# Spectral mixing and a gated FFN on one core: six table transfers put ahead of the weight loads, and row 8's fillers split

## The chip, the cores and the metric

The kernel runs on one core of one Trainium2 chip. The metric is the device time of one execution in microseconds (us), taken as the median of several runs. A profiled execution gives the trace: every instruction of the engines PE (matmuls, with the weight loads on PEld), DVE (VectorE), ACT (ScalarE) and POOL (GpSimd), and the issues of the DMA queue SP, on one clock that starts with the span.

## The reference

```python
def _A_ref(x, w_r, w_i):                       # x: 1 x 2048 x 576
    X = rfft2(x.astype(float32), axes=(-2, -1))
    X = X * (w_r + 1j * w_i)
    return irfft2(X, s=(S, D)).astype(bfloat16)

def _B_ref(x, w_gate, w_up, w_down):           # 576 -> 4608 -> 576
    return (gelu(x @ w_gate) * (x @ w_up)) @ w_down

h  = x + _A_ref(layernorm(x), w_r, w_i)
h2 = h + _B_ref(layernorm(h), w_gate, w_up, w_down)
```

Inputs and output are bfloat16. The Fourier transforms are done as matrix products with tables of sines and cosines that the kernel makes itself.

## The kernel before

The order of the instructions on every engine is the order of the source: nothing is rescheduled. Each engine works through its own list and waits, instruction by instruction, for what it reads and for the tile that it writes. The 2048 tokens lie in the 16 rows h of `h_sb` (128 partitions each). PSUM is used as four tiles of two banks each, taken in rotation (`two(name)`): a new tile waits until the readers of the tile four takes earlier are done.

The work falls into these stages:

1. **Rows.** DVE and ACT take the statistics of the 16 rows (`sd`, `ln_act`), POOL the reciprocal roots, DVE normalises a row into `xn` (L137), PE multiplies it with the row table `F16` (`row16`, L308, and `row16_rest`, L324). ACT and DVE cast the products from PSUM to `Bt` (`evict`, L335; `evict4`, L341). `small_table` (L404) makes a small PSUM tile `pt` out of `F16` and the identity; ACT copies it to `G16` later (L447), for use near the end of the spectral part. Ahead of rows 0 and 8 `row16` calls `fill`: matmuls of the identity with the first row of `h_sb` (L298), written to the PSUM bank that the row then overwrites. Nobody reads their result.
2. **Columns, and the way back along the tokens.** A loop over i, with the frequencies k in `order`: `f2` (L516) multiplies `Bt` with the column table `DT`, ACT casts the result (L527), `f3` (L533, L534) combines, DVE sums (`sum_of`, L566) and multiplies with the weights of the filter (`wmul`, L584 to L608) into `Zt`, and `i3` (L624, for k = 0 L648) transforms back along the tokens with the table `TI`, from where ACT (L632, L637, L656, L661) and in one place DVE (L656) write `EO`.
3. **Back along the columns.** `inv_cols(x, g)` (L675) multiplies `EO[x]` with the inverse column table: five steps w, each with two matmuls, one on the partitions from 0 up and one on those from 64 up. The latter read `DQ[64:, w]`, the former `DQ[0:, w]`, but for w = 0, where they read `DT` itself. ACT takes most of the results out (L692, L699), DVE two (L690, L697). `add_rows` (L811) adds the parts to rows of `h_sb`.
4. **The FFN.** `gate` (L939) multiplies the normalised rows with gate and up weights, then the down product (L982, L1001) follows, four times over 512 tokens. The first groups of weights, `pre`, are loaded while stage 2 runs.

All the transfers that the change speaks of go through one queue, SP, which issues them in the order of the source. `load_dq(1)` (seven transfers, SBUF to SBUF, source `DT`) fills the upper half of `DQ` at the end of stage 1. `load_dq(0)` (six transfers of 6.8 to 32.9 KB) fills the lower half; its call stands in the branch i = 2 of the loop of stage 2, in this order:

```python
cosine(rest)                                    # ACT
turn_tf(rest)                                   # SP: transposes TF into TI (L269)
pre = [load_gu(g) for g in range(3)]            # SP: wgu, six loads of 432 KB (L146)
load_dq(0)                                      # SP: six transfers (L484)
nc.sync.dma_start(wd_a[:], ...)                 # SP: 1728 KB (L734)
```

The next loads on SP are `wgu_e` (four of 432 KB), whose memory comes free when the last `i3` has read its tables.

On PE the last part of stage 2 and the first of stage 3 are interleaved: f3(0), inv_cols(0, 0) and (0, 1), i3(6), inv_cols(0, 2) to (0, 4), i3(7), inv_cols(0, 5) and (0, 6), i3(0), inv_cols(0, 7), inv_cols(1, 0) and so on (`order` is 1 to 7, then 0).

Of the kernel before, what the change touches and what calls it, by code (L numbers as in the profile page):

```python
# [42 lines left out]
def kernel_body(  # L43
# [23 lines left out]
    def two(name):  # L67
        return psum.tile([P, 2, 512], FP32, name=name, tag="two", bufs=4)
# [72 lines left out]
    def load_gu(g, t=None):  # L141
        gc = slice(g % (NFT // FQ) * FQ * P, (g % (NFT // FQ) + 1) * FQ * P)
        if t is None:
            t = wgpool.tile([P, NR, FQ * P], BF16, name="wgu", tag="wgu")[:]
        for c, w in ((0, B_w_gate), (1, B_w_up)):
            nc.sync.dma_start(t[64 * c : 64 * c + 64], w[:, gc].rearrange("(r k) c -> k r c", k=64))  # L146
        return t
# [105 lines left out]
    def angle_s(sl):  # L253
        V.tensor_scalar(ab[:, sl], pr[:, sl], -1024.0, None, op0=ALU.add)

    def angle_c(sl):
        drop_sign(ab[:, sl], ab[:, sl])

    def sine(sl):
        A.activation(TF[:, sl, 2, :], pr[:, sl], ACT.Sin, bias=pib[:], scale=-2.0 * PI / S)  # L260

    def cosine(sl):
        A.activation(TF[:, sl, 1, :], ab[:, sl], ACT.Sin, bias=nhpib[:], scale=2.0 * PI / S)

    def minus_sine(sl):
        V.tensor_scalar(TF[:, sl, 0, :], TF[:, sl, 2, :], -1.0, None, op0=ALU.mult)

    def turn_tf(sl):
        nc.sync.dma_start(  # L269
            TI[:, sl].rearrange("p k r q -> p (k r) q"), TF[:, sl].rearrange("p k r q -> p (k r q)"), transpose=True  # L270
        )
# [18 lines left out]
        V.tensor_scalar(F16[:, 2, :], F16[:, 0, :], -1.0, None, op0=ALU.mult)  # L290

    ps_f = {}
    FILL = {0: 16, 8: 12}

    def fill(dst, n):

        for _ in range(n):
            T.matmul(dst, lhsT=ident[:], rhs=h_sb[:, 0, 0:512], start=True, stop=True)  # L298

    def row16(h):  # L300
        if h % 2 == 0 or h == H - 1:
            ps_f[h] = two("f2t")
        f2t, b = (ps_f[h], 0) if h in ps_f else (ps_f[h - 1], 1)
        fill(f2t[:, b, :], FILL.get(h, 0))
        x = xn[:, h, :]
# [92 lines left out]
    pt = []  # L398

    def small_table():  # L400
        pt.append(two("pt"))
        for x in range(2):
            for p0 in (0, 64):
                T.matmul(  # L404
                    pt[0][p0 : p0 + 64, 0, x * P : (x + 1) * P],
                    lhsT=F16[:, 0, 64 * x : 64 * x + 64],
                    rhs=ident[:],
                    start=True,
                    stop=True,
                )  # L410
# [24 lines left out]
    norms(4, 8)  # L435
    rests(4)
    small_table()
    gather(1)
    sd(10, 12)
# [38 lines left out]
    def load_dq(r):  # L478
        for w in range(1 - r, NW):
            j0, j1 = w * JW, (w + 1) * JW  # L480
            for lo, hi in ((j0, min(j1, (j0 // P + 1) * P)), ((j0 // P + 1) * P, j1)):
                if lo < hi:
                    p0 = 64 * r + lo - j0
                    nc.sync.dma_start(  # L484
                        DQ[p0 : p0 + hi - lo, w], DT[lo % P : lo % P + hi - lo, lo // P, :, r, :]
                    )
# [22 lines left out]
    def f2(c):  # L509
        ps = two("pq_ps")  # L510
        col = slice(slot[c] * P, (slot[c] + 1) * P)
        steps = [(par, t) for par in range(2) for t in (par, par + 2, 4)]
        if c == order[0]:
            steps.sort(key=lambda s: s[1] == 4)
        for par, t in steps:
            T.matmul(  # L516
                ps[:, par, 0:JP],
                lhsT=Bt[:, t, col],
                rhs=DT[:, t // 2, par] if t < 4 else DF[:, par],
                start=(t == par),  # L520
                stop=(t == 4),
            )
        pq[c] = wk.tile([P, 2, JP], BF16, name="pq", tag="pq", bufs=6)
        pq_ps[c] = ps

    def f2_out(c, copy=A.copy, rs=slice(0, 2)):
        copy(  # L527
            pq[c][:, rs].rearrange("p r (j a) -> p r j a", a=2),
            pq_ps[c][:, :, 0:JP].rearrange("p a (r j) -> p r j a", r=2)[:, rs],
        )  # L530
# [5 lines left out]
    def f3(k, half):  # L536
        ps = two("gh_ps")
        if k == 0:
            p0, p8 = pq[0], pq[8]
            t0, t1 = (NS, C) if half else (C, SN)  # L540
            for b, kk, p in ((0, 0, p0), (1, 8, p8)):
                comb(ps[:, b, 0:J], kk, t0, p[:, 0, 0:J], t1, p[:, 1, 0:J])
            if half == 0:
                xab[k] = wk.tile([P, 2, 2, JP], BF16, name="xab", tag="xab", bufs=2)
            A.copy(xab[k][:, half, :, 0:J], ps[:, :, 0:J])
            return
        p, q = pq[k], pq[k + 8]
        gh = wk.tile([P, 2, JP], BF16, name="hs" if half else "g", tag="hs" if half else "g", bufs=2)
        r = half
        comb(ps[:, r, 0:J], k, C, p[:, r, 0:J], SN, q[:, r, 0:J])  # L550
        comb(ps[:, 1 - r, 0:J], k, C, q[:, r, 0:J], NS, p[:, r, 0:J])
        if k == order[0] and half:
            hk[k] = ps
            return
        A.copy(gh[:, :, 0:J], ps[:, :, 0:J])
        if half == 0:
            gk[k] = gh
            return
        hk[k] = gh

    def sum_of(k, half):
        g, hs = gk[k], hk[k]
        if half == 0:
            xab[k] = wk.tile([P, 2, 2, JP], BF16, name="xab", tag="xab", bufs=2)
        x = xab[k]
        V.tensor_tensor(  # L566
            x[:, 1, ::-1, 0:J] if half else x[:, 0, :, 0:J],
            g[:, :, 0:J],
            hs[:, :, 0:J],
            ALU.add if half else ALU.subtract,  # L570
        )
# [133 lines left out]
    for i in range(n + 1):  # L705
        last = i >= n
        if not last:
            f2(order[i])
            if i != 1:
                f2_out(order[i])  # L710
        if i == 0:
            f2(order[0] + 8)
            for r in range(2):
                f2_out(order[0] + 8, V.tensor_copy, slice(r, r + 1))
            angle_s(rest)
            angle_c(rest)
            sine(rest)

        if 1 <= i <= n:
            f3(order[i - 1], 0)  # L720
            f3(order[i - 1], 1)
            if i == 1:
                f2_out(order[1])
                minus_sine(rest)
                sum_of(order[0], 0)
                sum_of(order[0], 1)
                V.tensor_scalar(G16v[1], G16v[0], -1.0, None, op0=ALU.mult)
            else:
                if i == 2:
                    cosine(rest)  # L730
                    turn_tf(rest)
                    pre = [load_gu(g) for g in range(3)]
                    load_dq(0)
                    nc.sync.dma_start(wd_a[:], wd_view[:, 0:NWA, :])  # L734
                wmul(order[i - 2], i - 1, order[i - 1])
        if not last and i:
            f2(order[i] + 8)
            f2_out(order[i] + 8)
        if last:
            inv_cols(0, 0)  # L740
            inv_cols(0, 1)
        if i >= 3:
            for s in range(3):
                i3(order[i - 3], s)
        if last:
            wmul(order[i - 1], i)
        if i == 2:
            scr_pool.__exit__(None, None, None)
            eop = ctx.enter_context(tc.tile_pool(name="eop", bufs=1, side="right"))
            EO = [eop.tile([P, 5, H, 2, 4, 8], BF16, name=f"EO{x}", tag=f"EO{x}") for x in range(2)]  # L750
# [266 lines left out]
@with_exitstack  # L1017
def kernel(
    ctx: ExitStack,
    tc: tile.TileContext,  # L1020
    A_x: bass.AP,
    A_w_r: bass.AP,
    A_w_i: bass.AP,
    B_x: bass.AP,
    B_w_gate: bass.AP,
    B_w_up: bass.AP,
    B_w_down: bass.AP,
    out: bass.AP,
):
    kernel_body(tc, A_x, A_w_r, A_w_i, B_x, B_w_gate, B_w_up, B_w_down, out)  # L1030
# [30 lines left out]
```

## Time and profile before

| | |
|---|---|
| median of 3 runs | 503.55 us (502.54 to 503.64) |
| profiled execution, its time | 503.53 us |
| its span, first to last instruction | 501.7 us |
| mean granted TensorE clock | 0.992 |
| PE busy | 489.0 us |
| DVE, ACT, POOL busy | 223.9, 160.0, 28.3 us |
| first FFN matmul (L939) | at 74.19 us |

A line of the timeline reads: start in us, busy time in us, engine, source line, operation, output and inputs, shape, count; in square brackets the idle time of the engine ahead of it and what ended it. Several instructions of one kind in a row are merged into one line. SPq is SP's queue as it issues transfers: the landing is later.

### The profile page before, as it was taken

How to read it: one execution, taken by the hardware profiler on the slowest of the kernel's cores; microseconds unless marked ns; L12 is line 12 of the kernel's file. 1: busy time of each engine (PE TensorE's matmuls, PEld its weight loads, DVE VectorE, ACT ScalarE, POOL GpSimd, SP SyncE). 2: the span in 40 equal slices, each digit the busy share in tenths (PEclk: the TensorE clock that was granted, in tenths of full speed). 3: DMA queues.
4: the chain of work that ended last, by engine and by line, in shares of the span. 5: the costliest groups of instructions: out<-in, count | busy, mean ns of one | idle time of the engine just before them, and what ended most of it. 6: DMA issues, size and time to landing. Idle time of an engine off the chain costs nothing.

```text
span 501.7 us, 12760 instructions
## 1 busy us (share of the span) xinstructions
PE 489.0 (97%) x5714; PEld 340.9 (68%) x5714; DVE 223.9 (45%) x450; ACT 160.0 (32%) x284; POOL 28.3 (6%) x79
## 2 busy tenths in 40 slices
PE   7799799999999999999999999999999999999997
PEld 3578489886569975555589955555799655555995
DVE  7999566599751237633311155333212233333111
ACT  8899574332220113323210032323100232323000
POOL 8400000011110001100000000000000000000000
PEclk9999799999999999999999999999999999999999
DMA  8649566949993019987750069988700188770000
GB/s 277 209 88 205 158 137 160 194 100 198 198 230 69 1 50 173 192 160 160 159 104 2 3 130 189 205 155 159 154 5 3 53 164 159 158 151 6 13 14 24
DMA packets 89549, 62.33 MB, mean 124 GB/s; under 512 B 23190, under 2 KB 88086, under 8 KB 89494
## 3 DMA queue, kind: packets, MB, share of 16 engines
q1 hardware_dynamic: 89206, 60.34, 59.4%
q0 software_dynamic: 288, 1.18, 0.8%
q8 instruction: 44, 0.72, 0.6%
q14 instruction: 11, 0.09, 0.1%
HBM read 52.65 MB, written 2.36 MB: 110 GB/s over the span
## 4 chain that ended last, share of the span: by engine, by line
PE 89%; SPq 3%; DMA 1%; issue 0%; DVE 0%
PE gu L939 56%; PE acc L982 26%; PE cs_ps L675 2%; SPq L484 2%; PE acc L1001 2%; SPq L146 1%; PE y_ps L811 1%; PE eo_ps L624 1%; DMA DQ<-DT 1%; PE eo_ps L648 0%; PE pt L880 0%; PE pq_ps L516 0%; PE gh_ps L534 0%; DVE h_sb L1008 0%; SPq L269 0%
## 5 line engine op out<-in xcount | busy, mean ns | idle before, releaser
L939 PE MATMUL gu<-Bt,wgu 64*128 64x512 bf16 (+1 forms) x2646 | 270.6, 363 | 0.0
L939 PEld LDWEIGHTS <-wgu 64*128 64x128 bf16 x2646 | 152.5, 94 | 114.6 <-issue 0.3
L948 DVE TENSOR_TENSOR P_sb<-g_sb,gu 128x512 bf16<-128x512 f32 (+1 forms) x156 | 100.4, 645 | 140.3 <-ACT g_sb L947 140.3
L947 ACT ACTIVATE g_sb<-gu 128x512 f32<-128x512 f32 (+1 forms) x156 | 88.0, 564 | 193.5 <-PE gu L939 193.5
L982 PEld LDWEIGHTS <-P_sb 64*128 64x128 bf16 x2160 | 123.1, 94 | 9.9
L982 PE MATMUL acc<-wd,P_sb 64*128 64x288 bf16 x1440 | 90.9, 283 | 0.0
L991 DVE TENSOR_TENSOR part<-part,acc 128x576 f32<-128x576 f32 x15 | 11.3, 755 | 112.6 <-ACT part L990 112.6
L990 ACT COPY part<-acc 128x576 f32<-128x576 f32 x15 | 9.6, 639 | 122.8 <-PE acc L982 122.8
L982 PE MATMUL acc<-wd_a,P_sb 64*128 64x288 bf16 x720 | 46.8, 283 | 0.0
L675 PE MATMUL cs_ps<-DQ,EO 58*128 58x290 bf16 x144 | 13.4, 315 | 2.7 <-DMA DQ<-DT 2.7
L298 PE MATMUL f2t<-h_sb,ident 128*128 128x512 bf16 x28 | 9.2, 498 | 5.4 <-DMA h_sb<-in_A_x_dram 3.7
L675 PEld LDWEIGHTS <-EO 58*128 58x128 bf16 x160 | 8.4, 103 | 7.1 <-issue 3.4
L516 PE MATMUL pq_ps<-DT,Bt 128*128 128x290 bf16 x64 | 12.3, 286 | 1.0 <-ACT Bt L335 1.0
L939 PE MATMUL gu<-Bt,wgu_e 64*128 64x256 bf16 (+1 forms) x162 | 12.5, 305 | 0.0
L836 DVE TENSOR_SCALAR hrow<-h_sb,mv,rstd 128x1152 bf16<-128x1152 bf16 x14 | 12.2, 868 | 0.6 <-POOL rstd L874 0.6
L516 PEld LDWEIGHTS <-Bt 128*128 128x128 bf16 x96 | 9.2, 97 | 3.5 <-ACT Bt L335 1.1
L993 DVE TENSOR_TENSOR h_sb<-h_sb,part 128x576 bf16<-128x576 bf16 x15 | 11.4, 758 | 0.5
L134 POOL TENSOR_TENSOR rstd<-rstd,mhalf 128x1 f32<-128x1 f32 (+1 forms) x16 | 11.2, 699 | 1.3
L939 PEld LDWEIGHTS <-wgu_e 64*128 64x128 bf16 x162 | 10.3, 94 | 1.2
L133 POOL TENSOR_SCALAR rstd<-mv 128x1 f32<-128x1 f32 (+1 forms) x16 | 3.9, 243 | 116.9 <-DVE mv L119 115.9
L298 PEld LDWEIGHTS <-ident 128*128 128x128 bf16 x28 | 3.4, 121 | 10.3 <-issue 6.3
L527 ACT CAST pq<-pq_ps 128x580 bf16<-128x580 f32 x15 | 9.9, 666 | 0.4 <-PE pq_ps L516 0.2
(143 smaller groups left out, 283.6 us busy)
## 6 DMA issues: line engine op xcount, KB each, us to landing
wgu<-in_B_w_gate_dram SPq DMA_DIRECT2D x46, 432.0 KB
wgu<-in_B_w_up_dram SPq DMA_DIRECT2D x46, 432.0 KB
wd_a<-in_B_w_down_dram SPq DMA_DIRECT2D x1, 1728.0 KB
wd<-in_B_w_down_dram SPq DMA_DIRECT2D x1, 1728.0 KB
wd<-in_B_w_down_dram SPq DMA_DIRECT2D x6, 288.0 KB
out_dram<-h_sb SPq DMA_DIRECT2D x3, 576.0 KB
h_sb<-in_A_x_dram SPq DMA_DIRECT2D x4, 288.0 KB
h_sb<-in_A_x_dram SPq DMA_DIRECT2D x2, 576.0 KB
```

The source lines that it names most:

```text
L134: G.tensor_tensor(dst[:, sl], dst[:, sl], mhalf[:, sl], ALU.pow)
L298: T.matmul(dst, lhsT=ident[:], rhs=h_sb[:, 0, 0:512], start=True, stop=True)
L484: nc.sync.dma_start(DQ[p0 : p0 + hi - lo, w], DT[lo % P : lo % P + hi - lo, lo // P, :, r, :])
L516: T.matmul(ps[:, par, 0:JP], lhsT=Bt[:, t, col], rhs=DT[:, t // 2, par] if t < 4 else DF[:, par], start=(t == par), stop=(t == 4),)
L675: T.matmul(ps[:, e, 0:JP], lhsT=EO[x][rows, w, 2 * g : 2 * g + 2].rearrange("p h e k l -> p (h e k l)"), rhs=DQ[rows, w] if w or e else DT ...
L836: V.tensor_scalar(hrow[:], h_sb[:, h, :].rearrange("p (r k) -> p r k", k=64).unsqueeze(2).to_broadcast([P, NR, 2, 64]), mv2[:, h, 0:1], rs ...
L939: T.matmul(gu[:, c, 0:n], lhsT=w[rows, r, i * P : (i + 1) * P], rhs=hl[tcnk % 2][rows, r, lo:hi], start=(r == 0), stop=(r == NR - 1),)
L947: A.activation(g_sb, gu[:, 0, 0:n], ACT.Gelu_apprx_tanh)
L948: V.tensor_tensor(p_sb(f)[:, lo:hi], g_sb, gu[:, 1, 0:n], ALU.mult)
L982: T.matmul(accs[i][:, c, 0:DH], lhsT=p_sb(f)[rows, st * P : (st + 1) * P], rhs=wd[f // NWA][rows, f % NWA, c * DH : (c + 1) * DH], start=( ...
L991: V.tensor_tensor(part, part, accs[1][:, :, 0:DH], ALU.add)
L993: V.tensor_tensor(hv, hv, part, ALU.add)
```

## The change

Two edits that are independent of each other. `load_dq(0)` is called ahead of the three `load_gu` instead of behind them, so on SP the six transfers L484 stand directly behind the transposes of `turn_tf(rest)`, and the six loads of `wgu` behind them; `wd_a` follows as before. And row 8's twelve fillers become nine: six are called in `small_table`, written to the second bank of `pt` ahead of the four matmuls L404 (which use the first bank), and three stay ahead of row 8. Nothing else moves on any engine; the lines behind the first edit have numbers higher by one.

```diff
-    FILL = {0: 16, 8: 12}
+    FILL = {0: 16, 8: 3}
...
     def small_table():
         pt.append(two("pt"))
+        fill(pt[0][:, 1, :], 6)
         for x in range(2):
             for p0 in (0, 64):
                 T.matmul(
...
                     cosine(rest)
                     turn_tf(rest)
+                    load_dq(0)
                     pre = [load_gu(g) for g in range(3)]
-                    load_dq(0)
                     nc.sync.dma_start(wd_a[:], wd_view[:, 0:NWA, :])
```

## The prediction

> **What bounds the kernel now.** I read four views in this order: the chain that ended last, the waits of PE, the granted clock by stretches, and the timelines of the engines around the two edits. First the chain (start, duration, what):
>
> ```profile
> 51.59 2.88 DMA DQ<-DT
> ...
> 61.44 1.20 PE eo_ps L624 x10
> ...
> 63.99 1.24 PE eo_ps L648 x40
> ...
> 68.19 3.74 PE cs_ps L675 x60
> ...
> 74.45 27.46 PE gu L939 x468
> ```
>
> From 74.45 us on the FFN's matmuls are the chain, nearly without a break. Neither edit touches them, so all that can be won is that they begin sooner. Ahead of them the chain runs through a transfer of `DQ`: PE waited for the table's lower half. PE's own waits from 10 to 76 us (total, times, longest) and the stretches (length; then for PE, PEld, DVE, ACT, POOL the busy time; granted clock, DMA share, GB/s):
>
> ```profile
> PE cs_ps L675 <- DMA DQ<-DT: 2.7, 4, 1.6
> PE f2t L298 <- ACT Bt L335: 1.7, 1, 1.7
> PE pq_ps L516 <- ACT Bt L335: 1.0, 1, 1.0
> ```
>
> ```profile
> 14.20:18.80 4.60, 2.89 (x22) 1.43 (x18) 4.53 (x18) 3.67 (x6) 3.70 (x9) 1.00 0.86 295
> ...
> 32.40:50.40 18.00, 17.97 (x151) 14.57 (x150) 18.00 (x41) 17.18 (x30) 0.00 (x0) 1.00 1.02 187
> 50.40:54.50 4.10, 1.38 (x10) 0.41 (x8) 3.96 (x10) 1.33 (x3) 0.00 (x0) 0.91 0.45 80
> 54.50:61.00 6.50, 6.49 (x48) 3.81 (x50) 2.09 (x4) 3.77 (x6) 0.00 (x0) 0.53 0.71 249
> ```
>
> The waits for `DQ` sum to 2.7 us, but the price is larger. In the thin stretch from 50.40 to 54.50 PE is busy for 1.38 of 4.10 us, and the clock, 1.00 before, is 0.91 over it and 0.53 over the next 6.50 us, in which PE is full: it works there at half speed. Wait and slow clock together are the price, and I take it from the schedule, not by adding the two.
>
> **Edit 1, the six transfers.** The issues on SP (start, time taken to issue):
>
> ```profile
> 26.82 5.35 SPq L484 DMA_DIRECT2D DQ<-DT  x7
> 32.28 3.21 SPq L269 DMA_TRANSPOSE TI<-TF  x1
> ...
> 42.08 10.16 SPq L484 DMA_DIRECT2D DQ<-DT  x6
> ```
>
> [...] The seven of the upper half, with no weights ahead, took 5.35, or 0.76 each. In the new place they start when the transposes are issued, 32.28 + 3.21 = 35.49, take 6 x 0.76 = 4.6, and with the 2.88 of the chain behind the last issue they land at about 43; if they issued as slowly as now, at 48.5. PE first asks for them at 50.46 (below), so the cover is 2 to 7 us, and I cost them at nothing. They need nothing that is late: `DT` was last written in stage 1. What queues behind them on SP are the six loads of `wgu` and `wd_a`, each 4.6 us later; the rivals return to that.
>
> What is late next? Without the wait three engines could set the pace from 50.46 to the first `inv_cols(1, 0)`, which stands at 65.79 now:
>
> ```profile
> 50.46 0.29 PE L675 MATMUL cs_ps<-DQ,EO 58*128 58x290 bf16 x1
> ...
> 65.79 0.28 PE L675 MATMUL cs_ps<-DT,EO 58*128 58x290 bf16 x1
> ...
> 83.03 3.21 PE L939 MATMUL gu<-Bt,wgu_e 64*128 64x256 bf16 x54
> ```
>
> ```profile
> 50.52 1.21 ACT L545 CAST xab<-gh_ps 128x578 bf16<-128x578 f32 x2
> ...
> 62.45 1.01 ACT L632 CAST EO<-eo_ps 128x1024 bf16<-128x1024 f32 x1 [0.28 <-PE eo_ps L624]
> ...
> 63.63 0.72 ACT L692 ACTIVATE cw<-cs_ps 128x580 f32<-128x580 f32 x1
> 64.60 0.59 ACT L656 CAST EO<-eo_ps 128x512 bf16<-128x512 f32 x1 [0.25 <-PE eo_ps L648]
> 65.27 0.37 ACT L661 CAST EO<-eo_ps 128x256 bf16<-128x256 f32 x1
> ...
> 66.62 0.83 ACT L699 ACTIVATE cs<-cs_ps 128x580 bf16<-128x580 f32 x1
> ...
> 70.28 2.98 ACT L692 ACTIVATE cwb<-cs_ps 128x580 f32<-128x580 f32 x5
> ```
>
> PE at full clock: eight `inv_cols` at 3.74 / 6 = 0.62, two `i3` at 1.20, one at 1.24, together 8.6, so 50.46 + 8.6 = 59.1. ACT, which must empty these tiles in order: `xab` 1.21, two `cs` at 0.83, two pairs L632 and L637 at 63.63 - 62.45 = 1.18, four `cw` at 2.98 / 5 = 0.60, L656 0.59 and L661 0.37, together 8.6, so 50.52 + 8.6 = 59.1. DVE hands over the last `Zt` at 56.70 (its row is in the next part), after which 1.24 of `i3` and 0.62 of `inv_cols` follow, 58.6. PE and ACT end together; as PE also waits for one of four PSUM tiles now and then, I take 59.2. Edit 1 is worth 65.79 - 59.2 = 6.6 us. Its bounds: 7.2 if PE and ACT are a little shorter in a stream than in these rows, so that DVE's 58.6 sets the end, and 5.9 if handing over from PE to ACT and back costs another 0.1 at each of seven places.
>
> **Edit 2, the fillers.** The rows of PE, DVE and ACT in stage 1:
>
> ```profile
> 14.23 0.30 PE L404 MATMUL pt<-ident,F 128*64 128x128 bf16 x4
> 16.24 2.75 PE L298 MATMUL f2t<-h_sb,ident 128*128 128x512 bf16 x12 [1.71 <-ACT Bt L335]
> 18.83 1.91 PE L308 MATMUL f2t<-F,xn 128*128 128x256 bf16 x16
> ...
> 22.86 0.41 PE L324 MATMUL f<-F,xn 128*64 128x128 bf16 x8
> 24.27 0.67 PE L516 MATMUL pq_ps<-DT,Bt 128*128 128x290 bf16 x4 [0.99 <-ACT Bt L335]
> ```
>
> ```profile
> 17.06 1.40 DVE L137 TENSOR_SCALAR xn<-h_sb,mv,rstd 128x576 bf16<-128x576 bf16 x4
> ...
> 19.49 1.44 DVE L137 TENSOR_SCALAR xn<-h_sb,mv,rstd 128x576 bf16<-128x576 bf16 x4
> ...
> 22.07 0.31 DVE L463 COPY DF<-DT 32x580 bf16<-32x580 bf16 x1
> 23.32 0.69 DVE L341 CAST Bt<-f 128x512 bf16<-128x512 f32 x1 [0.94 <-PE f L324]
> ...
> 56.24 0.46 DVE L608 TENSOR_TENSOR Zt<-m,m 128x580 bf16<-128x580 bf16 x1
> ```
>
> ```profile
> 17.46 0.41 ACT L447 ACTIVATE G<-pt 128x256 bf16<-128x256 f32 x1
> 19.90 1.93 ACT L335 CAST Bt<-f2t 128x1024 bf16<-128x1024 f32 x2 [2.03 <-PE f2t L308]
> ...
> 22.19 2.02 ACT L335 CAST Bt<-f2t 128x1024 bf16<-128x1024 f32 x3
> ```
>
> A filler costs (18.83 - 16.24) / 12 = 0.216. Six of them now stand at 14.23, where the tile `pt` is free (the table's matmuls start there today), and end at 15.5, the table at 15.9. ACT copies `pt` only at 17.46, so the delay of 1.3 costs nothing. The remaining three wait, as the twelve did, for row 8's PSUM tile until 16.24 and end at 16.9. Row 8 needs its `xn`, the first of four at 17.06 + 0.35, so PE starts it at 17.5 and not at 18.83: the last six fillers were no cover, they held the row up for 1.3. From there: rows 8 to 11 and their rests 1.9 + 0.4 to 19.8; row 12's `xn` comes at 19.49 + 0.36, so it starts at 19.95 and the last rest ends at 22.2, now 22.86 + 0.41 = 23.27. DVE's cast L341 then waits for DVE alone, 22.07 + 0.31 = 22.38, and starts at 22.4 for 23.32: 0.9 of the idle 0.94. ACT casts row 8 at 18.5, and its last cast follows row 15 (21.9): with the three casts spread over the rows and 2.02 / 4 for a single one, it ends at 23.0 for 24.2. So `f2` could start 1.1 sooner, but the angles, the first `pq` halves and all sums behind L341 are DVE's, which has no gap from 32.40 to 50.40 (18.00 busy of 18.00). The smaller figure passes: 0.9 up to the last `Zt`, `turn_tf(rest)` and the six transfers included. Bounds: 0, if another input of stage 2 is as late as L341, and 0.94, DVE's whole idle; I take 0.9, nearest to the row. Below 0 I see nothing: no instruction is added, three are gone, and none moves behind a later one.
>
> **The sum.** 6.6 + 0.9 = 7.5 us off the profiled execution's 503.53 us (span 501.7, so 1.8 outside it, unchanged): 496.0. The median, 503.55, is the same within 0.02. FFN start: 74.2 - 7.5 = 66.7.
>
> **Rivals.** *Only edit 1 counts:* 503.5 - 6.6 = 496.9. For it: stage 2 starts off several inputs at once. Against: the 0.94 in DVE's row is its only idle time there that a row on PE ends.
>
> *The clock falls all the same.* With the wait gone, PE, ACT and four PSUM tiles cycle at equal pace, with short idles on PE; a thin stretch could again halve the clock. One cold stretch of the length seen (about 6.8 us: from the end of 50.40:54.50, where 0.91 leaves 0.7, to 61.0 less 0.4) costs half of it, 3.4: 499.4. Against: from 32.40 to 50.40 the same four tiles cycle with ACT busy for 17.18 of 18.00, at 1.00; and at 14.20:18.80, with PE busy for only 2.89 of 4.60, the clock held too. [...] I give it 0.05.
>
> *The table is late anyway.* If the six stick behind the transposes in the queue, PE waits again, and only edit 2 and a part remain: 499 to 502.6 (503.5 - 0.9). It decides if they take more than 2 to 7 us longer than I reckon. Against: the upper half also followed transposes, and its first part was there at 50.46 without a wait.
>
> *Slower: the weights are late.* `wgu` and `wd_a` (six of 432 KB, 1728 KB) now start 3.7 later (4.6 less 0.9), and `wgu_e` (four of 432 KB) queues behind them. All are 6.2 MB; at the 187 GB/s of 32.40:50.40 that is 33 us from 39.2, so 72.3. The first use of `wgu_e` moves from 83.03 to 75.5: 3 us of slack, more since one of its two groups is enough to start. To end over 504.5, the transfers must land 8.5 us after that use, at 84, a rate of 138 GB/s. Against: 249 GB/s stood at 54.50:61.00. 0.03.
>
> **Chances and range.** Forecast 0.80; only edit 1 0.08; clock 0.05; table late 0.03; weights late 0.03; nothing moves, 503.5, 0.01. The forecast's own bounds run from 503.5 - 7.2 - 0.94 = 495.4 to 503.5 - 5.9 - 0.6 = 497.0; the runs' spread of 1.1 adds half a microsecond at each end, and with the first rival at 496.9 that makes 494.9 to 497.9, 0.88 of the cases less what the spread leaves out. The measurement can tell about 0.2%, 1.0 us. Faster by more: all but two of the cases, 0.95; the same 0.02; slower 0.03.
>
> **What would show it.** Right: in the profile after, L485's six issues stand directly behind the transposes and take about 4.6 us; PE has no wait for `DQ`; the clock is 1.00 from 50 to 61; L308 for row 8 starts near 17.5, DVE's cast L341 near 22.4; `inv_cols(1, 0)` at 58.3, the first L940 at 66.7. Wrong: a wait of PE on ACT of over 1 us in stage 3, a clock of half there, a wait of PE for `wgu` or `wgu_e`, or L341 at its old place.

## The result, and the profile after

The changed kernel takes 496.37 us (median of 4 runs, 495.88 to 496.45) against 503.58 before (4 runs); the ratio is 0.9859, 95% interval 0.9842 to 0.9877. Beside 16 runs of the kernel before on one chip it took 496.28 against 502.69, ratio 0.9871 (0.9856 to 0.9886). The forecast was 496.0, with 494.9 to 497.9 as its range. The profiled execution's span went from 501.7 to 494.6 us.

These are all the waits of PE from 10 to 70 us after (total in us, times, longest). The wait for `DQ` is gone, and nothing is left of the wait of the fillers for ACT:

```profile
PE f2t L308 <- DVE xn L137: 1.6, 3, 0.9
PE pq_ps L517 <- ACT Bt L335: 0.9, 1, 0.9
PE gh_ps L534 <- ACT TF L263: 0.3, 1, 0.3
PE gh_ps L535 <- ACT pq L528: 0.2, 1, 0.2
```

The stretches after are set 0.9 us earlier than those shown of before (length; busy time of PE, PEld, DVE, ACT, POOL; granted clock, DMA share, GB/s). PE is full, and at clock 1.00. Before it was busy for 1.38 of 4.10 us there and then ran at a mean of 0.53 over 6.50 us:

```profile
49.50:53.60 4.10, 4.10 (x55) 2.90 (x55) 3.96 (x9) 4.10 (x9) 0.00 (x0) 1.00 1.13 203
53.60:60.00 6.40, 6.40 (x116) 4.87 (x112) 3.79 (x7) 5.69 (x10) 0.00 (x0) 1.00 1.08 308
```

The issues on SP after. The six stand directly behind the transposes and take 4.44 us for 10.16; the first weight load starts at 39.75:

```profile
31.72 3.49 SPq L269 DMA_TRANSPOSE TI<-TF  x1
35.26 4.44 SPq L485 DMA_DIRECT2D DQ<-DT  x6
39.75 0.70 SPq L146 DMA_DIRECT2D wgu<-in_B_w_gate_dram  x1
```

PE in stage 1 and at the end of the spectral part, then DVE and ACT. The small table follows the six fillers at 15.81, three more fillers start at 16.14, and row 8 now waits for DVE alone:

```profile
14.41 1.47 PE L298 MATMUL pt<-h_sb,ident 128*128 128x512 bf16 x6
15.81 0.30 PE L405 MATMUL pt<-ident,F 128*64 128x128 bf16 x4
16.14 0.81 PE L298 MATMUL f2t<-h_sb,ident 128*128 128x512 bf16 x3
17.81 1.92 PE L308 MATMUL f2t<-F,xn 128*128 128x256 bf16 x16 [0.86 <-DVE xn L137]
...
23.42 0.67 PE L517 MATMUL pq_ps<-DT,Bt 128*128 128x290 bf16 x4 [0.87 <-ACT Bt L335]
```

```profile
49.66 0.29 PE L676 MATMUL cs_ps<-DT,EO 58*128 58x290 bf16 x1
...
58.62 0.28 PE L676 MATMUL cs_ps<-DT,EO 58*128 58x290 bf16 x1
...
67.00 9.11 PE L940 MATMUL gu<-Bt,wgu 64*128 64x256 bf16 x162
```

```profile
17.38 1.40 DVE L137 TENSOR_SCALAR xn<-h_sb,mv,rstd 128x576 bf16<-128x576 bf16 x4
...
22.73 0.69 DVE L341 CAST Bt<-f 128x512 bf16<-128x512 f32 x1
...
55.59 0.46 DVE L609 TENSOR_TENSOR Zt<-m,m 128x580 bf16<-128x580 bf16 x1
```

The first `inv_cols(0, 0)` starts at 49.66 for 50.46, `inv_cols(1, 0)` at 58.62 for 65.79, the FFN at 67.00 for 74.2. Between the first two points lie 8.96 us after and 15.33 before. These 6.37 us come from edit 1, and the 0.80 us by which the first point moved from edit 2, as the kernels with one edit alone bear out below.

### The profile page after: what moved, and what is told of

It is laid out like the page before. It is cut to its first block, busy times and chain, and to the rows that moved or that the text cites. A ratio compares the mean times of both kernels' runs of the same rounds, so it can differ in the third digit from the quotient of the medians.

```text
span 494.6 us, 12754 instructions
## 1 busy us (share of the span) xinstructions
PE 484.7 (98%) x5711; PEld 338.8 (69%) x5711; DVE 224.2 (45%) x450; ACT 159.2 (32%) x284; POOL 29.0 (6%) x79
## 4 chain that ended last, share of the span: by engine, by line
PE 93%; DVE 0%; issue 0%
PE gu L940 57%; PE acc L983 27%; PE cs_ps L676 2%; PE acc L1002 2%; PE eo_ps L625 2%; PE pq_ps L517 1%; PE y_ps L812 1%; PE gh_ps L535 1%; PE gh_ps L534 1%; PE eo_ps L649 0%; PE pt L881 0%; DVE h_sb L1009 0%
## 5 line engine op out<-in xcount | busy, mean ns | idle before, releaser
L940 PE MATMUL gu<-Bt,wgu 64*128 64x512 bf16 (+1 forms) x2646 | 270.6, 363 | 0.0
L940 PEld LDWEIGHTS <-wgu 64*128 64x128 bf16 x2646 | 152.3, 94 | 114.8 <-issue 0.3
L940 PE MATMUL gu<-Bt,wgu_e 64*128 64x256 bf16 (+1 forms) x162 | 12.5, 305 | 0.0
L940 PEld LDWEIGHTS <-wgu_e 64*128 64x128 bf16 x162 | 10.3, 94 | 1.3
L676 PE MATMUL cs_ps<-DQ,EO 58*128 58x290 bf16 x144 | 10.8, 283 | 0.0
L298 PE MATMUL f2t<-h_sb,ident 128*128 128x512 bf16 x19 | 6.4, 506 | 3.8 <-DMA h_sb<-in_A_x_dram 3.7
L308 PE MATMUL f2t<-F,xn 128*128 128x256 bf16 x64 | 7.7, 273 | 1.7 <-DVE xn L137 1.6
```

What stands on the lines that cost most here:

```text
L676: T.matmul(ps[:, e, 0:JP], lhsT=EO[x][rows, w, 2 * g : 2 * g + 2].rearrange("p h e k l -> p (h e k l)"), rhs=DQ[rows, w] if w or e else DT ...
L940: T.matmul(gu[:, c, 0:n], lhsT=w[rows, r, i * P : (i + 1) * P], rhs=hl[tcnk % 2][rows, r, lo:hi], start=(r == 0), stop=(r == NR - 1),)
```

## The experiments

**Both edits, and each alone.** The three kernels ran on one chip, beside 16 runs of the kernel before.

> The changed kernel once more, beside its parts on the same chip. Both theories: 496.4 us, 7.2 below the kernel before; no wait of PE for DQ, clock 1.00 from 49 to 61 us. Whether DVE's cast L341 again starts at 22.7 (0.6 earlier than before) or at the forecast 22.4 (0.9 earlier) tells if the missing 0.3 comes with the arrival of the input x in one execution or with the edit.

> Edit 1 alone: the six transfers ahead of the weights, the twelve fillers as before. Theory, the two edits are independent and add up: 6.5 of the 7.2 us, 497.1 us, with row 8 starting near 18.8 and L341 near 23.3 as before. Rival, edit 1 carries all of it and the fillers are nothing: 496.4 us, the same as both edits.

> Edit 2 alone: the fillers split, the transfers behind the weights as before. Theory, stage 2 starts 0.6 to 0.9 us earlier and takes the weights' issue and so the six transfers along: 502.7 to 503.0 us, with the wait for DQ and the half clock behind it unchanged in length. Rival, the wait for DQ swallows it because the transfers land when the weights let them: 503.6 us, PE's wait for DQ longer by 0.6 to 0.9 us.

The diffs of this section are against the changed kernel, but for that of e3, which is against the kernel before.

```diff
 e1:
-    FILL = {0: 16, 8: 3}
+    FILL = {0: 16, 8: 12}
...
-        fill(pt[0][:, 1, :], 6)
 e2:
-                    load_dq(0)
                     pre = [load_gu(g) for g in range(3)]
+                    load_dq(0)
```

| kernel | median us (runs) | ratio to before, 95% |
|---|---|---|
| before | 502.69 (16) | |
| both edits | 496.28 (4) | 0.9871 (0.9856 to 0.9886) |
| edit 1 alone | 497.02 (5) | 0.9894 (0.9879 to 0.9909) |
| edit 2 alone | 502.54 (11) | 0.9990 (0.9981 to 0.9999) |

Edit 1 alone gives 5.7 of the 6.4 us; edit 2 adds 0.7 to it, but alone only 0.15. In the traces edit 2 brings row 8 and the cast L341 forward, as forecast, both alone and beside edit 1. DVE's rows of both edits (first two), then of edit 1 alone:

```profile
16.96 1.40 DVE L137 TENSOR_SCALAR xn<-h_sb,mv,rstd 128x576 bf16<-128x576 bf16 x4
...
22.31 0.69 DVE L341 CAST Bt<-f 128x512 bf16<-128x512 f32 x1
```

```profile
17.25 1.40 DVE L137 TENSOR_SCALAR xn<-h_sb,mv,rstd 128x576 bf16<-128x576 bf16 x4
...
23.21 0.69 DVE L341 CAST Bt<-f 128x512 bf16<-128x512 f32 x1 [0.64 <-PE f L324]
```

With edit 2 the cast follows the normalising by 5.35 us in both executions (16.96 to 22.31, 17.38 to 22.73). DVE is without a gap between the two, and the missing 0.3 of the first profile after is where that chain began: DVE had waited for a part of the input x until 7.51 us there, and until 6.55 in the profile of both edits. Without edit 2 the cast stands at 23.2 to 23.3 in four profiles, held by PE, with the normalising starting anywhere from 17.06 to 17.43. So the gain of edit 2 differs with the arrival of x.

Why is it lost when it stands alone? Stage 2 does start sooner, and PE reaches `DQ` 1.0 us sooner (49.44 for 50.46). But the transfers move by less: the last is issued from 51.1 us on for 51.6. So the wait grows, from 2.7 to 3.3 us:

```profile
PE cs_ps L676 <- DMA DQ<-DT: 3.3, 4, 2.1
```

```profile
49.50:54.70 5.20, 1.86 (x21) 0.85 (x20) 5.06 (x11) 1.57 (x4) 0.00 (x0) 1.00 0.48 101
54.70:58.10 3.40, 3.40 (x24) 1.96 (x22) 1.03 (x3) 2.42 (x4) 0.00 (x0) 0.50 1.08 383
```

The second row of the stretches shows something else: the half clock lasted 3.4 us in this execution, not 6.8. That led to the next two runs.

**Wait and clock apart.**

> The kernel before with one addition: 18 fillers of 0.216 us, 3.9 us together, ahead of inv_cols(0, 0), where PE waits for DQ. Transfers and row 8's fillers as before. Theory, half of edit 1's gain is the wait and half the clock that falls after it: PE stays busy, the clock stays at 1.00, inv_cols(1, 0) comes 3 to 3.5 us earlier than at 65.8, and the time is about 500.2 us. Rival, the clock falls for another reason than the thin stretch on PE (the transfers, or the work itself): the granted clock is 0.5 from 54 to 61 us again, and the time is 503.6 us or more.

```diff
         ps = two("cs_ps")
+        if x == 0 and g == 0:
+            fill(ps[:, 1, :], 18)
         for w in range(NW):
```

The time was 501.09 us (6 runs), ratio 0.9968 (0.9956 to 0.9980). PE's rows and the stretches of this run, then two rows of edit 1 alone:

```profile
50.32 4.04 PE L298 MATMUL cs_ps<-h_sb,ident 128*128 128x512 bf16 x17
54.29 0.29 PE L677 MATMUL cs_ps<-DT,EO 58*128 58x290 bf16 x1
...
63.24 0.28 PE L677 MATMUL cs_ps<-DT,EO 58*128 58x290 bf16 x1
```

```profile
49.50:53.60 4.10, 4.05 (x23) 2.09 (x22) 3.96 (x10) 2.13 (x4) 0.00 (x0) 1.00 0.42 74
53.60:60.00 6.40, 6.40 (x74) 4.25 (x72) 2.89 (x6) 4.63 (x8) 0.00 (x0) 1.00 0.87 279
```

```profile
50.34 0.29 PE L675 MATMUL cs_ps<-DT,EO 58*128 58x290 bf16 x1
...
59.29 0.28 PE L675 MATMUL cs_ps<-DT,EO 58*128 58x290 bf16 x1
```

The clock held at 1.00 in all six runs, with the transfers as late as before: the six are issued from 42.18 us on for 42.08. Only the thin stretch is gone, PE being busy for 4.05 of 4.10 us and not for 1.38. So it is this stretch behind which the clock falls here, and the rival is out. But the gain was 1.6 us by the medians, not the 3.4 behind the forecast of 500.2. The rest of edit 1's gain, 501.09 - 497.02 = 4.1, is the time for which the fillers stood in the way: the stretch starts at 54.29 and not at edit 1's 50.34.

That is a little more than the wait itself. Two of the runs of the kernel before in the table below kept the full clock and took 500.50 and 500.72 us, some 0.5 us less than this kernel, so the fillers lasted longer than the wait that they covered. By these two runs, which ran on other chips, 3.6 us of edit 1's 5.7 are wait and 2.1 are clock.

> The kernel before, once more, for another profile of the slow stretch behind the wait for DQ. [...] Rival, it is fixed by the kernel's own pattern: again 6.8 us, from 53.8 to 60.6 us.

This was the unchanged kernel: 503.2 us (one run), with the half clock (0.51) for 6.9 us again, as the rival had it, but 0.9 us earlier than in the first profile, so its place is not fixed. The rows of this run, then the one of the first profile of before:

```profile
50.40:52.80 2.40, 0.63 (x5) 0.20 (x4) 2.37 (x6) 1.30 (x3) 0.00 (x0) 1.00 0.26 44
52.80:59.70 6.90, 5.83 (x36) 3.02 (x38) 3.66 (x8) 2.95 (x4) 0.00 (x0) 0.51 0.83 266
```

```profile
53.70:60.60 6.90, 6.51 (x44) 3.60 (x45) 2.89 (x6) 3.63 (x5) 0.00 (x0) 0.51 0.77 254
```

The mean granted clock over the execution is known for every run. Over the 43 runs of the kernel before that stand beside these experiments it falls into four groups, each with its own time:

| mean granted clock | runs of before | us |
|---|---|---|
| 1.000 | 2 | 500.50, 500.72 |
| 0.997 | 25 | 501.87 to 502.97 |
| 0.993 or 0.992 | 15 | 503.08 to 504.51 |
| 0.990 | 1 | 504.84 |

By estimate a mean lower by 0.0035 over some 500 us is 3.5 us at half clock; by the table each such step costs 1 to 2 us. The profiles agree: 3.4 us at 0.50 in the executions with a mean of 0.997 (edit 2 alone, and e4 below), 6.9 us at 0.51 in those with 0.992 and 0.993 (before, and this run). What sets the length of a step, no run shows. The half clock of the first profile, two steps long, was not the usual case: by their mean clock 25 of 43 runs lost one.

That also explains edit 2 alone. Of its 11 runs 8 are at 0.992 or 0.993 (502.22 to 502.95) and 3 at 0.997 (501.59 to 501.87); within each group it is some 0.7 us below the kernel before, which had 7 of its 16 runs beside it at 0.992 or 0.993. So the small gain alone fits a clock that more often lost two steps behind the longer wait; 11 runs against 16 are too few to call that rate shown.

**What the fillers guard.**

> The changed kernel without any of the nine fillers around row 8. PE then does 0.3 us of work between about 14.4 and 17.5 us. Theory, the fillers hold the clock: a stretch this thin lets it fall as the one at 50 us did, rows 8 to 15 run at half speed, DVE's cast L341 comes up to 4 us later, and the time is 497 to 500 us, differing from run to run. Rival, they hold nothing up and guard nothing: granted clock 1.00, 496.3 us as the changed kernel.

```diff
-    FILL = {0: 16, 8: 3}
+    FILL = {0: 16}
...
-        fill(pt[0][:, 1, :], 6)
```

```profile
14.50:18.40 3.90, 0.75 (x15) 0.55 (x10) 3.87 (x15) 3.34 (x6) 3.44 (x9) 1.00 0.82 289
18.40:21.80 3.40, 3.40 (x23) 2.14 (x22) 3.33 (x12) 1.72 (x2) 1.55 (x5) 0.50 0.99 292
```

The time was 497.36 us (4 runs), 1.1 more than with the nine. By the mean clock (0.996 or 0.997) the clock fell for one step in three of the four runs, and the one that kept 1.000 took 496.0. The fillers do hold the clock, and the rival falls. The nine are enough: in the 13 runs of the changed kernel (the first result and its two repeats) the mean was 0.999 or 1.000. One of the five runs of edit 1 alone stood at 0.997 and took 498.79 us; where it lost a step no profile shows.

**How early the table must be, and how late the weights may be.**

> The changed kernel with the six transfers behind the first two of the three weight groups. Theory, the gain is all or nothing by the landing: two groups (four loads of 432 KB) at 187 GB/s take 9.5 us from about 35, so the six land at 48 to 50 us, just about when PE asks at 49.5; PE's wait for DQ is under 1 us, the clock stays at 1.00, and the time is 496.3 to 497.3 us. Rival, each load ahead costs its share: two thirds of edit 1's 5.7 us are lost again, 500 us.

> The changed kernel with wd_a (1728 KB) put ahead of the three weight groups too, which makes wgu about 9 us later still. Theory, the FFN's weights have that much cover: wgu lands by 63 us at 187 GB/s or sooner and is first used at 67; no wait of PE at L940, 496.3 us. Rival, the weights were close to late (the case in which the change would have lost time): PE waits at the first L940 and the time is 499 us or more.

```diff
 e5:
-                    load_dq(0)
-                    pre = [load_gu(g) for g in range(3)]
+                    pre = [load_gu(g) for g in range(2)]
+                    load_dq(0)
+                    pre.append(load_gu(2))
 e6:
                     load_dq(0)
-                    pre = [load_gu(g) for g in range(3)]
                     nc.sync.dma_start(wd_a[:], wd_view[:, 0:NWA, :])
+                    pre = [load_gu(g) for g in range(3)]
```

The changed kernel did not run beside these two and the one without fillers. The kernel before took 502.63 us (7 runs) beside them and 502.69 beside the first three, so their times can be set next to each other, but a difference of one or two tenths is not clear.

Behind two groups the time was 496.05 us (4 runs), as good as ahead of all three. The six took 9.53 us to issue again, and PE's first nine matmuls on them took 0.93 us where the changed kernel's take 0.80. PE's weight loads wait for `DQ` once, for 0.3 us, and in the changed kernel not at all. So the six landed only just in time, and a share of the loads costs no share of the gain.

```profile
38.12 9.53 SPq L485 DMA_DIRECT2D DQ<-DT  x6
```

```profile
49.32 0.93 PE L676 MATMUL cs_ps<-DQ,EO 58*128 58x290 bf16 x9
```

```profile
PEld L676 <- DMA DQ<-DT: 0.3, 1, 0.3
```

With `wd_a` ahead of the weights the time was 496.53 us (4 runs), with no wait of PE for a weight and the first L940 at 67.16. From the first `inv_cols` to there it is 17.77 us, for 17.34 in the changed kernel. Most of this 0.4 lies near 58 us, where PE has idle moments for which the profile names no releaser; their cause stays open:

```profile
58.78 0.42 PE L676 MATMUL cs_ps<-DQ,EO 58*128 58x290 bf16 x4 [0.16 <-issue]
```

**A better version?** With the fillers out of the way I took DVE for the bound of stage 1, and gave it less to do.

> The changed kernel with 1.7 us of DVE work taken out from ahead of the cast L341: the two copies to DF (0.31 each) go to POOL, and the three angle steps of the first two frequencies (1.1 us) move behind the last rows' normalising. Theory, with the fillers out of the way DVE alone sets when stage 2 starts: rows 12 to 15 and L341 come earlier, L341 by 0.3 to 0.6 us against the start of the third L137, and the time falls by 0.3 to 0.6 us, to 495.7 to 496.0 beside the changed kernel's 496.3 in the same call. Rival, PE or ACT is as late as DVE there, or POOL's copies are slow: L341 starts but f2 does not, and the time stays within 0.2 us or rises.

> The changed kernel once more, as the measure for the kernel beside it: 496.3 us, granted clock 1.00.

> The changed kernel with the last cast L341 (0.69 us) given from DVE to ACT, behind ACT's own casts, and the angle steps of the first two frequencies behind the last normalising, so that PE and ACT come earlier. The copies to DF stay on DVE. Theory, DVE sets the start of stage 2 now: its angles (L237) start 0.7 us or more sooner, ACT has the time since it waits for PE and DVE there (0.21 and 0.44 us), and the time falls by 0.3 to 0.6 us to 495.7 to 496.0. Rival, ACT's queue is as tight: the sines of the first frequencies and the first pq come later by the 0.6 us of the cast, and the time is 496.3 or more.

> The same cast on ACT, the angle steps where they were. Theory, without the move PE ends row 15 later, ACT's casts and the one added end 0.5 us later, and of the gain 0.1 to 0.3 us is left: 496.0 to 496.2. Rival as for the kernel beside it: 496.3 us or more.

```diff
 e9 and e11:
+    norms(12, 16)
+    rests(12)
     angle_b(first)
     angle_s(first)
     angle_c(first)
-    norms(12, 16)
-    rests(12)
...
 e9:
-    V.tensor_copy(DF[0:32], D3[0:32])
-    V.tensor_copy(DF[96:128], D3[96:128])
+    G.tensor_copy(DF[0:32], D3[0:32])
+    G.tensor_copy(DF[96:128], D3[96:128])
 e11 and e12:
-        (V.tensor_copy if h == 12 else A.copy)(
+        A.copy(
```

The changed kernel again took 496.25 us (5 runs). With the copies on POOL (e9) it was 496.70 (5 runs, one of them 498.98 at a mean clock of 0.997; a sixth took 1323.87, and no profile shows why). With the cast on ACT it was 496.25 (e11) and 496.11 (e12), 5 runs each. The gain forecast for e9 and e11, to 495.7 to 496.0, did not come. POOL is too slow, 0.66 and 1.61 us for copies that cost DVE 0.31 (spans on POOL are rough), and PE waits 0.7 us for the second:

```profile
21.94 0.66 POOL L463 COPY DF<-DT 32x580 bf16<-32x580 bf16 x1 [3.28 <-ACT Bt L335]
22.66 1.61 POOL L464 COPY DF<-DT 32x580 bf16<-32x580 bf16 x1
```

```profile
PE pq_ps L517 <- POOL DF L464: 0.7, 1, 0.7
```

Taking the cast off DVE moves nothing that can be measured: PE starts `f2` when ACT's casts end, as it did, and ACT has the cast on top (rows of e11, PE and ACT):

```profile
23.34 0.67 PE L517 MATMUL pq_ps<-DT,Bt 128*128 128x290 bf16 x4 [0.99 <-ACT Bt L335]
```

```profile
23.12 0.65 ACT L341 CAST Bt<-f 128x512 bf16<-128x512 f32 x1
```

None of these, nor e5, is clearly faster than the changed kernel's own 496.25 to 496.37, and e9 is slower: its five runs lie above all five of the changed kernel beside it.

## Why the prediction was right, step by step

**The six transfers** were costed at nothing, with 4.6 us to issue. They took 4.44, and PE did not wait. The cover was real, and e5 shows its end.

**What is late next.** 59.2 was forecast for `inv_cols(1, 0)` from a start at 50.46, 8.74 later. It is 8.96 later in the profile after, and 8.95 in edit 1 alone and in e3. The term was 0.2 too short. PE and ACT were to end together: both are full in the first stretch above, 4.10 of 4.10, but in the second PE is busy for 6.40 of 6.40 and ACT for 5.69. So by the end PE alone sets the pace. The missing time lies mostly where PE goes from `inv_cols` to `i3`: at these three places an `inv_cols` takes 0.71 or 0.72 us from its start to that of `i3`, and not the 0.62 of the sum. Edit 1 in the profile: 6.6 forecast, 6.37 measured.

**Edit 2.** Row 8 at 17.81 (forecast 17.5), L341 at 22.73 (22.4): late by the 0.3 of x's arrival, on time in the second profile (22.31). But the step "the smaller figure passes" failed: L341 moved by 0.59 and the last `Zt` by 0.65, while PE's start of `f2` moved by 0.85 and `inv_cols(0, 0)` by 0.80. It is the path of ACT's casts and PE that passes, the one I had put aside as the larger. From the start of `f2` to `inv_cols(0, 0)` it is 26.18 to 26.24 us in the profiles of before, after, both edits again and edit 1 alone, so with edit 2 or without; that the cast taken off DVE gave nothing fits this. The path begins at DVE all the same: in all three profiles of the changed kernel `f2` starts 6.04 us behind the first L137 for row 8, by way of PE's rows and ACT's casts.

**The sum** of 7.5 was 7.1 on the spans of the two profiles and 7.2 by the first medians. It was 6.4 beside 16 runs of before: to take the median for "the same within 0.02" was too trusting. The profile of before, and by their times two of the three runs shown, had lost two steps of the clock; the usual run loses one. The forecast of the time, 496.0, does not suffer from this, since it takes off only what that one execution had lost. That the gain came out at 7.2 at first was chance. So edit 1's 6.4 in the profile is 5.7 in the medians, of which 3.6 to 4.1 are wait and 1.6 to 2.1 clock, as two runs of before and e3 have it.

The wait alone is more than the 2.7 of the wait's row. Rows of before:

```profile
52.33 0.30 PE L675 MATMUL cs_ps<-DQ,EO 58*128 58x290 bf16 x2 [1.57 <-DMA DQ<-DT]
...
53.85 0.42 PE L675 MATMUL cs_ps<-DQ,EO 58*128 58x290 bf16 x2 [0.54 <-DMA DQ<-DT]
...
54.73 0.45 PE L675 MATMUL cs_ps<-DT,EO 58*128 58x290 bf16 x1
```

The second `inv_cols` starts at 54.73, 4.27 us behind the first, where it takes 0.64 after: 3.6 us of wait. A pair of matmuls in the thin stretch is shown as busy for 0.30 us (0.42 at half clock), while the five pairs of an `inv_cols` take 0.62 in a stream. Idle time before an instruction leaves out what such a stretch wastes.

The range was added up loosely. Its upper end takes 0.6 for edit 2, for which no row is given, where the bound named was 0; and 497.0 with half a microsecond more is 497.5, not 497.9. In the profile edit 2 was worth 0.80.

**The rivals.** *Only edit 1*: no, edit 2 adds 0.7 to it. *The clock falls all the same*: no run of the changed kernel shows it. In the profiles the clock fell only behind stretches in which PE was busy for 19 to 36% of the time (0.75 of 3.90 us in e4, 0.63 of 2.40 in e7, 1.38 of 4.10 before, 1.86 of 5.20 with edit 2 alone). In the changed kernel, with four PSUM tiles in turn, PE is busy for 4.10 of 4.10 and 6.40 of 6.40 us, at clock 1.00. *Table late* and *weights late*: no, with room to spare for the weights, as e6 shows. For the table there is less: with two groups ahead the room is gone.

## What to carry to other kernels

A small transfer that is needed soon does not belong behind a queue of large ones that are needed late (here the six took 10.16 us to issue behind them and 4.44 ahead of them): look at when each is asked for, not at when it is issued, and check with one displaced version how much room the order leaves. Price a wait of PE from the place where the schedule resumes, not from its idle row, and price the clock behind it from many runs, since how long it is down differs from run to run (here 0 to 3 steps of some 3.5 us, by the mean clock of 43 runs). Dummy matmuls that bridge a gap pay only up to the moment when the real work could start: here the last of twelve held up the work (row 8 started at 18.83 us, and at 17.81 with three), and with none at all the clock fell in three of four runs.

## What the runs showed of the hardware

In four profiles the clock fell to half (0.50 or 0.51) for 3.4 us or 6.9 us, at a place that differs from run to run (in the kernel before from 53.7 us on, and from 52.8 in e7). The same program took 500.5 to 504.8 us, and by an estimate from the mean clock of its runs it lost 0, 1, 2 or 3 steps of some 3.5 us. Issuing a small transfer took 0.74 us on SP with no weights ahead of it, and 1.7 us on average (the longest 3.75) behind six loads of 432 KB, although nothing on SP waited for a semaphore there; why, no row shows. DVE's copy of 32 partitions by 580 elements took 0.31 us, POOL's 0.66 and 1.61 beside a busy DVE.
